# Transposing q and k of batches 3 to 7 through DRAM rows, with loads, shifted copies of v and outputs moved to other queues

## The chip, the cores and the metric

One core of one Trainium2 chip. The metric is the device time of one execution in microseconds (us), as the median of a kernel's runs. The kernel before takes 342.97 us in the first three runs (341.77 to 344.68) and between 341.6 and 343.2 us in the groups of runs used below. Every experiment ran on one chip together with runs of the kernel before. A run is called slow when its time is over 1.5% above the fastest of the same kernel; ratios are of fast runs alone, and differences that only slow runs show are not used. The engines are called PE (TensorE), DVE (VectorE), ACT (ScalarE) and POOL (GpSimd); SP (SyncE) only issues transfers here.

## The reference

Sliding-window attention over 8 batches of 8 heads, 576 positions, head size 64, window 32, and then a two-layer network with an ELU on the 4608 resulting rows:

```python
scores = scale * np.matmul(q, k.transpose(0, 1, 3, 2))     # q, k, v: 8 x 8 x 576 x 64, float32
scores = np.where(np.abs(pos[:, None] - pos[None, :]) <= 32, scores, -1e9)
attn = softmax(scores)
x = np.matmul(attn, v).transpose(0, 2, 1, 3).reshape(4608, 512)
h = x @ w_in                                               # 512 x 2048
out = np.where(h > 0, h, np.exp(np.minimum(h, 0)) - 1) @ w_out
```

## The kernel before

The kernel works in 144 steps. A step is 8 matmuls of the first product and 4 of the second; in the steady part four steps carry one pair of attention blocks (scores, mask, product with v, division by the sums, and a transposing DMA of the result `x_st` into `xT`). The scores are computed from q and k with the head dimension on the partitions (`qT`, `kT`). In the kernel before, TensorE puts them so: a batch's q is loaded as float32 (`f`), cast to bfloat16 (`qkb`), transposed in groups of six (`ptx`) and copied to `qT` or `kT`.

```python
    def load_qk(b, which, part):                 # 1152 KB for a whole q or k of a batch
        ...
        nc.sync.dma_start(out=t[...], in_=(q, k)[which][b, ...])

    def load_v(b, m):                            # five per batch
        nc.gpsimd.dma_start(out=V_e[b % 3][...], in_=v[b, ...])

    def rotate_v(b, m0=0, m1=VS - 1):            # Vo is Ve shifted by 64 partitions
        nc.sync.dma_start(out=o[0:64, m0:m1], in_=e[64:128, m0:m1])
        nc.sync.dma_start(out=o[64:128, m0:m1], in_=e[0:64, m0 + 1:m1 + 1])

    def x_dma(i):                                # 28 pairs; the first 8 use TensorE
        nc.sync.dma_start_transpose(out=xT_of(i), in_=x_st...)
    ...
    for i in range(8, NPAIR):
        kk = 24 if i == 8 else HALF * (i - 2) - 2        # HALF is 4
        at(kk, "mid", scores, i)
        ...
        at(kk + 2, "end", x_dma, i)
    for b in range(2, B):
        k0 = HALF * (first_pair(b) - 2)
        for n in range(2 * HP):
            ...                                          # for b >= 3:
            which, hp = n % 2, n // 2
            kk, ahead = k0 - 16 + HALF * hp + which, 5
            at(kk - ahead, "mid", cast_qk, b, which, WHOLE, (hp,), nc.gpsimd)
            at(kk, "mid", transpose_qk, b, which, WHOLE, (hp,), nc.scalar)
        at(k0 - HALF, "mid", rotate_v, b)
        if b >= 3:
            kk = max(k0 - 8 * HALF, 18)
            at(kk, "mid", load_qk, b, 0, WHOLE)
            at(kk + 1, "mid", load_qk, b, 1, WHOLE)
            for m in range(VS):
                at(kk + 2 + m // 3, "mid", load_v, b, m)
    ...
        if s == STEPS - 1:                               # end of a tile of 256 rows
            nc.scalar.copy(y_sb[:, 0, :], psY[t][0])
            nc.vector.tensor_copy(y_sb[:, 1, :], psY[t][1])
            nc.sync.dma_start(out_t[t], y_sb)
```

`at(step, slot, ...)` puts a task into an engine's program at that step. It is an order, not a time: an engine with nothing to wait for runs ahead of it (in the changed kernel POOL sends out eight transfers, placed at different steps, between 93.45 and 100.08 us).

The softmax here doesn't subtract the row's maximum and nothing guards it: scores larger than these inputs give would overflow.

Of the kernel before, what the change touches and what calls it, by code (L numbers as in the profile page):

```python
# [10 lines left out]
BF16 = mybir.dt.bfloat16  # L11
# [10 lines left out]
def kernel(  # L22
# [9 lines left out]
    nc = tc.nc  # L32
# [13 lines left out]
    SP_ = S // SJ  # L46
    VS = 5
    VD = D + 1
    KW = S + 2 * WIN

    TT = 256
    NT = N_TOK // TT
# [13 lines left out]
    xpool = ctx.enter_context(tc.tile_pool(name="xT", bufs=4))  # L66
    mpool = ctx.enter_context(tc.tile_pool(name="moe", bufs=3))
    opool = ctx.enter_context(tc.tile_pool(name="outs", bufs=2))


    psum = ctx.enter_context(
# [14 lines left out]
        return pools[tag].tile(shape, dt, tag=tag, name=name)  # L86

    qT = [cpool.tile([128, HP, S], BF16, name=f"qT{i}") for i in range(2)]
    kT = [cpool.tile([128, HP, KW], BF16, name=f"kT{i}") for i in range(2)]
    V_e = [cpool.tile([128, VS, H, VD], BF16, name=f"Ve{i}") for i in range(3)]  # L90
    V_o = [cpool.tile([128, VS - 1, H, VD], BF16, name=f"Vo{i}")
           for i in range(3)]
# [6 lines left out]
    WHOLE, HALF_A, HALF_B = (0, SJ), (0, SJ // 2), (1, SJ // 2)  # L99
    qk_f = {}  # L100

    def load_qk(b, which, part):
        z, nj = part
        if (b, which) not in qk_f:
            qk_f[b, which] = lpool.tile([SP_, H * SJ * D], FP32,
                                        tag=f"f{which}", name=f"f{which}")
        t = qk_f[b, which]
        n = H * nj * D
        nc.sync.dma_start(
            out=t[:, z * n:(z + 1) * n].rearrange("p (h x) -> p h x", h=H),  # L110
            in_=(q, k)[which][b, :, z * SP_ * nj:(z + 1) * SP_ * nj, :]
            .rearrange("h (p j) d -> p h (j d)", j=nj))
# [6 lines left out]
            out=V_e[b % 3][p0:p1, m, :, 0:D],  # L119
            in_=v[b, :, lo + p0:lo + p1, :].rearrange("h p d -> p h d"))  # L120

    def rotate_v(b, m0=0, m1=VS - 1):
        e, o = V_e[b % 3], V_o[b % 3]
        nc.sync.dma_start(out=o[0:64, m0:m1], in_=e[64:128, m0:m1])
        nc.sync.dma_start(out=o[64:128, m0:m1], in_=e[0:64, m0 + 1:m1 + 1])

    gate_t = cpool.tile([1, 8], BF16, name="gate_t")
    gates = [0]
# [23 lines left out]
    for i in range(3):  # L152
        nc.vector.memset(V_e[i][:, :, :, D:VD], 1.0)
        nc.vector.memset(V_e[i][0:32, 0], 0.0)
        nc.vector.memset(V_e[i][96:128, VS - 1], 0.0)
        if i < 2:
            nc.vector.memset(kT[i][:, :, 0:WIN], 0.0)
            nc.vector.memset(kT[i][:, :, KW - WIN:KW], 0.0)

    ident = cpool.tile([128, 128], BF16)  # L160
    make_identity(nc, ident)
# [47 lines left out]
    def cast_qk(b, which, part, hps, eng):  # L209
# [8 lines left out]
        qk_b[b, which, z, hp0] = t  # L218
        copy_on(eng, _bap(t, [t.ap[0], [D, nh], [nh * D, nj], [1, D]]), s_)

    def transpose_qk(b, which, part, hps, evac, tag="t0"):
        z, nj = part
        src = qk_b.pop((b, which, z, hps[0]))
        nh = len(hps)
        W = 512 if nh > 1 else 1024
        pt = ps_tile([128, nh, W], BF16, tag, "ptx")
        for g in range(nh):
            for j in range(nj):
                nc.tensor.transpose(  # L229
                    pt[:, g, j * SP_:(j + 1) * SP_],  # L230
                    src[:, j, g * 128:(g + 1) * 128], ident[0:SP_, 0:SP_])
        n = SP_ * nj
        if which == 0:
            T, c0 = qT[b % 2], z * n
        else:
            T, c0 = kT[b % 2], WIN + z * n
        d = T[:, hps[0]:hps[0] + nh, c0:c0 + n]
        pitch = d.ap[1][0] if nh > 1 else n
        copy_on(evac,
                _bap(d, [d.ap[0], [pitch, nh], [nj, SP_], [1, nj]]),  # L240
                _bap(pt, [pt.ap[0], [W, nh], [1, SP_], [SP_, nj]]))
# [3 lines left out]
    def scores(i, tag="s"):  # L245
        psS = ps_tile([128, 2, 512], FP32, tag, "psS")
        for z in range(2):
            jb = 2 * i + z
            b, qb = jb // NQB, jb % NQB
            for h in range(H):  # L250
                hp, base = h // 2, 64 * (h % 2)
                nc.tensor.matmul(  # L252
                    psS[:, h % 2, hp * 128 + z * QB:hp * 128 + (z + 1) * QB],
                    lhsT=kT[b % 2][base:base + 64, hp, QB * qb:QB * qb + 128],
                    rhs=qT[b % 2][base:base + 64, hp, QB * qb:QB * (qb + 1)],
                    start=True, stop=True)
        pu = apool.tile([128, H, 2 * QB], BF16, tag="pu")
# [113 lines left out]
    def at(kk, slot, fn, *args):  # L371
        tasks.setdefault((kk, slot), []).append((fn, args))
# [40 lines left out]
        at(kk + 2, "end", x_dma, i)  # L413
    for b in range(2, B):
        k0 = HALF * (first_pair(b) - 2)
        for n in range(2 * HP):
            if b == 2:
                which, hp, kk, ahead = n // HP, n % HP, 18 + n, 2
            else:
                which, hp = n % 2, n // 2  # L420
                kk, ahead = k0 - 16 + HALF * hp + which, 5
            at(kk - ahead, "mid", cast_qk, b, which, WHOLE, (hp,), nc.gpsimd)
            at(kk, "mid", transpose_qk, b, which, WHOLE, (hp,), nc.scalar)
        at(k0 - HALF, "mid", rotate_v, b)
        if b >= 3:
            kk = max(k0 - 8 * HALF, 18)
            at(kk, "mid", load_qk, b, 0, WHOLE)
            at(kk + 1, "mid", load_qk, b, 1, WHOLE)
            for m in range(VS):
                at(kk + 2 + m // 3, "mid", load_v, b, m)  # L430



# [32 lines left out]
    def mm2(kk):  # L466
# [13 lines left out]
        if s == STEPS - 1:  # L480
            y_sb = opool.tile([128, 2, D_MODEL], FP32, tag="y_sb")
            nc.scalar.copy(y_sb[:, 0, :], psY[t][0])
            nc.vector.tensor_copy(y_sb[:, 1, :], psY[t][1])  # L483
            nc.sync.dma_start(out_t[t], y_sb)

    LAG = 2
    for kk in range(NSTEP + LAG):
# [40 lines left out]
```

## Time and profile before

| | kernel before |
|---|---|
| time, median | 342.97 us |
| span of the profiled run | 339.9 us |
| TensorE (PE) busy | 91%, at full granted clock (1.00 in each window of the prediction) |
| PE's waits for a transfer after 30 us | none over 0.3 us |

The page, the windows and the timeline that bound the kernel are shown in the prediction. Two more views matter for what came of it. First PE's waits (engine, line, what it waited for: us in total, times, longest):

```profile
PE ptx L229 <- DVE qkb L207: 12.5, 4, 7.0
...
PE psS L279 <- DMA Vo<-Ve: 1.9, 1, 1.9
```

Both lie in the start-up. Second, the page's DMA issues (count, size of one, median us from issue to landing):

```profile
f<-in_q_dram SPq DMA_DIRECT2D x6, 1152.0 KB, 9.8
...
Vo<-Ve SPq DMA_DIRECT2D x12, 260.0 KB, 4.0
Ve<-in_v_dram POOLq DMA_DIRECT2D x24, 128.0 KB, 10.9
```

Loads of q and k, the copies `Vo<-Ve` (below: Vo copies), outputs and x transposes are all issued by SP, in program order. SP's timeline (start, duration of the issue, what) shows what that does. I read over it before I predicted:

```profile
98.58 1.19 SPq L317 DMA_TRANSPOSE xT<-x_st  x1
99.87 0.53 SPq L109 DMA_DIRECT2D f<-in_q_dram  x1
106.87 1.19 SPq L317 DMA_TRANSPOSE xT<-x_st  x1
108.15 0.53 SPq L109 DMA_DIRECT2D f<-in_k_dram  x1
```

The program asks for the q load and the k load one step (2 us) apart, but SP stands at an x transpose until `x_st` is there (14 waits, 85.7 us). So in batches 4 and 5 each load leaves 1.3 us after the start of an x transpose's issue, and k 7.9 to 8.3 us after q, behind the next. In batches 6 and 7 that holds for k, which leaves 5.5 to 5.8 us after q; q leaves behind an output, 4.2 to 4.5 us ahead of the next x transpose. Batch 3's two leave at 70.70 and 71.21 us, ahead of all x transposes.

### The profile page before, as it was taken

How to read it: one execution, taken by the hardware profiler on the slowest of the kernel's cores; microseconds unless marked ns; L12 is line 12 of the kernel's file. 1: busy time of each engine (PE TensorE's matmuls, PEld its weight loads, DVE VectorE, ACT ScalarE, POOL GpSimd, SP SyncE). 2: the span in 40 equal slices, each digit the busy share in tenths (PEclk: the TensorE clock that was granted, in tenths of full speed). 3: DMA queues.
4: the chain of work that ended last, by engine and by line, in shares of the span. 5: the costliest groups of instructions: out<-in, count | busy, mean ns of one | idle time of the engine just before them, and what ended most of it. 6: DMA issues, size and time to landing. Idle time of an engine off the chain costs nothing.

```text
span 339.9 us, 8051 instructions
## 1 busy us (share of the span) xinstructions
PE 308.7 (91%) x3296; PEld 207.4 (61%) x3296; DVE 246.2 (72%) x446; ACT 167.3 (49%) x262; POOL 84.3 (25%) x108
## 2 busy tenths in 40 slices
PE   0347999799799999999999999999999999999994
PEld 0235666566566666666666666666666666666662
DVE  5346667678787777778877888788867777878663
ACT  1624264566545554555555554555555553444331
POOL 8352410085661344034400354021100000000000
PEclk9999999999999999999999999999999999999999
DMA  8999999999998995771949994963202320202011
GB/s 163 187 227 214 218 169 185 218 305 214 131 143 173 216 119 121 174 168 23 188 65 206 178 158 83 225 155 80 79 18 78 80 79 17 77 17 80 15 64 62
DMA packets 79176, 45.67 MB, mean 134 GB/s; under 512 B 53796, under 2 KB 73252, under 8 KB 79140
## 3 DMA queue, kind: packets, MB, share of 16 engines
q1 hardware_dynamic: 37412, 36.25, 47.4%
q0 software_dynamic: 41728, 8.92, 37.9%
q8 instruction: 26, 0.43, 0.6%
q14 instruction: 10, 0.08, 0.1%
HBM read 36.70 MB, written 9.44 MB: 136 GB/s over the span
## 4 chain that ended last, share of the span: by engine, by line
PE 83%; DVE 7%; DMA 4%; ACT 3%; issue 1%; SPq 0%; DVEq 0%
PE ps L447 36%; PE psY L474 35%; PE ptx L229 5%; PE psS L279 4%; PE psS L252 3%; DMA f<-in_k_dram 2%; DVE g_sb L460 2%; DMA Vo<-Ve 2%; DVE m_sb L455 1%; ACT e_sb L453 1%; DVE x_st L291 1%; ACT pu L258 1%; ACT qkb L205 1%; DVE pm L267 1%; DVE xT L313 1%
## 5 line engine op out<-in xcount | busy, mean ns | idle before, releaser
L453 ACT ACTIVATE e_sb<-ps 128x512 f32<-128x512 f32 x144 | 86.0, 597 | 152.1 <-PE ps L447 151.9
L447 PE MATMUL ps<-xT,w_in_sb 128*128 128x256 bf16 x1152 | 150.5, 274 | 4.1 <-DVE xT L313 3.3
L474 PE MATMUL psY<-w_out_sb,g_sb 128*128 128x512 bf16 x576 | 148.0, 379 | 0.2 <-DVE g_sb L460 0.2
L447 PEld LDWEIGHTS <-w_in_sb 128*128 128x128 bf16 x1152 | 110.2, 98 | 41.2 <-issue 4.8
L455 DVE TENSOR_SCALAR m_sb<-e_sb 128x512 bf16<-128x512 f32 x144 | 71.9, 500 | 59.2 <-ACT e_sb L453 58.8
L460 DVE SCALAR_TENSOR_TENSOR g_sb<-ps,m_sb 128x512 bf16<-128x512 f32 x144 | 99.4, 690 | 13.0
L474 PEld LDWEIGHTS <-g_sb 128*128 128x128 bf16 x576 | 50.8, 98 | 38.0 <-DVE g_sb L460 0.7
L207 POOL CAST qkb<-f 96x768 bf16<-96x768 f32 x48 | 41.3, 883 | 120.0 <-DMA f<-in_q_dram 40.0
L118 POOL DMA_DIRECT2D Ve<-in_v_dram x40 | 34.8, 875 | 28.1 <-PE psS L279 13.6
L229 PE MATMUL ptx<-ident,qkb 96*128 96x96 bf16 x384 | 27.7, 215 | 15.0 <-DVE qkb L207 12.5
L258 ACT ACTIVATE pu<-psS 128x1024 bf16<-128x1024 f32 x36 | 36.5, 1019 | 2.7 <-PE psS L252 2.6
L229 PEld LDWEIGHTS <-qkb 96*128 96x128 bf16 x384 | 23.5, 102 | 17.3 <-DVE qkb L207 13.0
L267 DVE TENSOR_TENSOR pm<-pu,masks 128x1024 bf16<-128x1024 bf16 x36 | 26.0, 721 | 2.0 <-ACT pu L258 1.7
L291 DVE TENSOR_TENSOR x_st<-psS,rc 128x512 bf16<-128x512 f32 x36 | 24.9, 692 | 1.2
L279 PEld LDWEIGHTS <-pm 128*64 128x64 bf16 x576 | 12.5, 113 | 17.3 <-DVE pm L267 13.4
L205 ACT COPY qT<-ptx 128x576 bf16<-128x576 bf16 (+1 forms) x30 | 20.0, 666 | 4.1 <-PE ptx L229 4.1
L252 PE MATMUL psS<-qT,kT 64*128 64x64 bf16 x576 | 15.3, 196 | 2.7 <-DVE x_st L291 1.2
L205 ACT COPY kT<-ptx 128x576 bf16<-128x576 bf16 (+1 forms) x26 | 17.4, 671 | 0.0
L252 PEld LDWEIGHTS <-kT 64*128 64x128 bf16 x576 | 11.2, 98 | 10.2 <-issue 7.7
L279 PE MATMUL psS<-Ve,pm 128*64 128x65 bf16 x320 | 16.5, 200 | 0.9 <-ACT pu L258 0.6
L279 PE MATMUL psS<-Vo,pm 128*64 128x65 bf16 x256 | 14.5, 200 | 2.0 <-DMA Vo<-Ve 1.9
L483 DVE COPY y_sb<-psY 128x512 f32<-128x512 f32 x18 | 12.4, 687 | 2.2 <-PE psY L474 1.8
(29 smaller groups left out, 55.1 us busy)
## 6 DMA issues: line engine op xcount, KB each, us to landing
out_dram<-y_sb SPq DMA_DIRECT2D x18, 512.0 KB, 2.9
f<-in_q_dram SPq DMA_DIRECT2D x6, 1152.0 KB, 9.8
f<-in_k_dram SPq DMA_DIRECT2D x6, 1152.0 KB, 9.4
Vo<-Ve SPq DMA_DIRECT2D x12, 260.0 KB, 4.0
Ve<-in_v_dram POOLq DMA_DIRECT2D x24, 128.0 KB, 10.9
f<-in_q_dram SPq DMA_DIRECT2D x4, 576.0 KB, 10.3
f<-in_k_dram SPq DMA_DIRECT2D x4, 576.0 KB, 12.0
w_in_sb<-in_moe_w_in_dram POOLq DMA_DIRECT2D x4, 512.0 KB, 19.2
```

Of the source, the lines that this page charges most:

```text
L118: nc.gpsimd.dma_start(out=V_e[b % 3][p0:p1, m, :, 0:D], in_=v[b, :, lo + p0:lo + p1, :].rearrange("h p d -> p h d"))
L205: nc.scalar.copy(d_, s_)
L207: eng.tensor_copy(d_, s_)
L229: nc.tensor.transpose(pt[:, g, j * SP_:(j + 1) * SP_], src[:, j, g * 128:(g + 1) * 128], ident[0:SP_, 0:SP_])
L252: nc.tensor.matmul(psS[:, h % 2, hp * 128 + z * QB:hp * 128 + (z + 1) * QB], lhsT=kT[b % 2][base:base + 64, hp, QB * qb:QB * qb + 128], rh ...
L258: nc.scalar.activation(pu, _bap(psS, [psS.ap[0], [1, 1024]]), AX.Exp, scale=SCALE)
L279: nc.tensor.matmul(psS[QB * z:QB * (z + 1), par, hp * VD:(hp + 1) * VD], lhsT=pm[:, par * HP + hp, z * QB:(z + 1) * QB], rhs=vv[:, qb // 2 ...
L447: nc.tensor.matmul(ps[:, j, :], lhsT=w_in_sb[:, do, fo * 128:(fo + 1) * 128], rhs=xT[t][:, :, do, :], start=(do == 0), stop=(do == NDO - 1))
L453: nc.scalar.activation(e_sb, ps, AX.Exp)
L455: nc.vector.tensor_scalar(m_sb, e_sb, -1.0, None, ALU.add)
L460: nc.vector.scalar_tensor_tensor(g_sb, psH.pop(kk), 0.0, m_t.pop(kk), ALU.max, ALU.min)
L474: nc.tensor.matmul(psY[t][ts], lhsT=g_sb[:, j, ts * 128:(ts + 1) * 128], rhs=w_out_sb[:, s * FG + j, :], start=(s == 0 and j == 0), stop=( ...
```

## The change

The intent is to take the q and k transposes of batches 3 to 7 off TensorE, which bounds the kernel (91% busy). ACT casts `f` to rows in bfloat16 and writes them to DRAM; SP brings them back with a transposing DMA. To keep SP's queue free for transposes, loads of q and k and Vo copies go to POOL's queue, and outputs and row writes to ACT's. ACT also takes over DVE's half of the copies of a finished tile to `y_sb`. (Recorded texts say "output copies" of either: where they go to POOL or hold up a transpose, Vo copies are meant.)

```diff
-    def load_qk(b, which, part):
+    def load_qk(b, which, part, eng=nc.sync):
...
+    def cast_rows(b, which, hp):
+        ...
+        nc.scalar.copy(...)                      # rows <- f, two heads
+    def write_rows(b, which):
+        ...
+        nc.scalar.dma_start(out=t.rearrange("(p j) c -> p j c", j=SJ), in_=rows.pop((b, which)))
+    def transpose_rows(b, which):
+        nc.sync.dma_start_transpose(out=keys_or_queries(b, which), in_=in_dram.pop((b, which)))
...
     for b in range(2, B):
         k0 = HALF * (first_pair(b) - 2)
         ...                                      # b == 2 stays as before
+        k0 -= 2
+        c0 = k0 - (19 if b == 3 else 23)
+        for which in range(2):
+            at(max(c0 - 7, 17) if which == 0 else c0 + 1, "mid",
+               load_qk, b, which, WHOLE, nc.gpsimd)
+            for hp in range(HP):
+                at(c0 + 8 * which + (0, 1, 4, 5)[hp], "end", cast_rows, b, which, hp)
+            at(c0 + 8 * which + 6, "mid", write_rows, b, which)
+            at(c0 + 8 * which + 8, "mid", transpose_rows, b, which)
+        for m in range(VS):
+            at(k0 - 20 + 2 * m, "mid", load_v, b, m)
+        at(k0 - 4, "mid", rotate_v, b, 0, VS - 1, nc.gpsimd)
...
-            nc.vector.tensor_copy(y_sb[:, 1, :], psY[t][1])
-            nc.sync.dma_start(out_t[t], y_sb)
+            nc.scalar.copy(y_sb[:, 1, :], psY[t][1])
+            nc.scalar.dma_start(out_t[t], y_sb)
```

Not shown: `kT` gets one row of positions with padding at its ends, so that one transpose can fill it.

More of the change, by code (lines that the diff above doesn't have):

```diff
@@ L48 @@
     VD = D + 1
-    KW = S + 2 * WIN
     TT = 256
@@ L68 @@
     opool = ctx.enter_context(tc.tile_pool(name="outs", bufs=2))
+    dpool = ctx.enter_context(
+        tc.tile_pool(name="dram", bufs=2, space=bass.MemoryType.DRAM))
     psum = ctx.enter_context(
@@ L88 @@
     qT = [cpool.tile([128, HP, S], BF16, name=f"qT{i}") for i in range(2)]
-    kT = [cpool.tile([128, HP, KW], BF16, name=f"kT{i}") for i in range(2)]
+    KPAD = 2 * WIN
+    kT = [cpool.tile([128, KPAD + HP * S + KPAD], BF16, name=f"kT{i}")
+          for i in range(2)]
     V_e = [cpool.tile([128, VS, H, VD], BF16, name=f"Ve{i}") for i in range(3)]
@@ L108, in load_qk @@
         n = H * nj * D
-        nc.sync.dma_start(
+        eng.dma_start(
             out=t[:, z * n:(z + 1) * n].rearrange("p (h x) -> p h x", h=H),
@@ L120, in load_v, with rotate_v @@
             in_=v[b, :, lo + p0:lo + p1, :].rearrange("h p d -> p h d"))
-    def rotate_v(b, m0=0, m1=VS - 1):
+    def rotate_v(b, m0=0, m1=VS - 1, eng=nc.sync):
         e, o = V_e[b % 3], V_o[b % 3]
-        nc.sync.dma_start(out=o[0:64, m0:m1], in_=e[64:128, m0:m1])
-        nc.sync.dma_start(out=o[64:128, m0:m1], in_=e[0:64, m0 + 1:m1 + 1])
+        eng.dma_start(out=o[0:64, m0:m1], in_=e[64:128, m0:m1])
+        eng.dma_start(out=o[64:128, m0:m1], in_=e[0:64, m0 + 1:m1 + 1])
     gate_t = cpool.tile([1, 8], BF16, name="gate_t")
@@ L156 @@
         if i < 2:
-            nc.vector.memset(kT[i][:, :, 0:WIN], 0.0)
-            nc.vector.memset(kT[i][:, :, KW - WIN:KW], 0.0)
+            for c0, n in ((KPAD - WIN, HP), (KPAD + HP * S, 1)):
+                z = kT[i][:, c0:c0 + WIN]
+                nc.vector.memset(_bap(z, [z.ap[0], [S, n], [1, WIN]]), 0.0)
     ident = cpool.tile([128, 128], BF16)
@@ L219, in cast_qk, with keys_or_queries @@
         copy_on(eng, _bap(t, [t.ap[0], [D, nh], [nh * D, nj], [1, D]]), s_)
+    def keys_or_queries(b, which):
+        if which == 0:
+            return qT[b % 2]
+        return kT[b % 2][:, KPAD:KPAD + HP * S].rearrange(
+            "p (g s) -> p g s", g=HP)
+    rows, in_dram = {}, {}
+    def cast_rows(b, which, hp):
+        if hp == 0:
+            rows[b, which] = lpool.tile([SP_, SJ, H * D], BF16,
+                                        tag=f"r{which}", name="rows", bufs=1)
+        n = SJ * D
+        s_ = qk_f[b, which][:, 2 * hp * n:(2 * hp + 2) * n]
+        d_ = rows[b, which][:, :, 2 * hp * D:(2 * hp + 2) * D]
+        nc.scalar.copy(
+            _bap(d_, [d_.ap[0], [D, 2], [H * D, SJ], [1, D]]),
+            _bap(s_, [s_.ap[0], [n, 2], [D, SJ], [1, D]]))
+    def write_rows(b, which):
+        t = dpool.tile([S, H * D], BF16, tag=f"d{which}", name="in_dram")
+        in_dram[b, which] = t
+        nc.scalar.dma_start(
+            out=t.rearrange("(p j) c -> p j c", j=SJ), in_=rows.pop((b, which)))
+    def transpose_rows(b, which):
+        nc.sync.dma_start_transpose(
+            out=keys_or_queries(b, which), in_=in_dram.pop((b, which)))
     def transpose_qk(b, which, part, hps, evac, tag="t0"):
@@ L232, in transpose_qk @@
         n = SP_ * nj
-        if which == 0:
-            T, c0 = qT[b % 2], z * n
-        else:
-            T, c0 = kT[b % 2], WIN + z * n
-        d = T[:, hps[0]:hps[0] + nh, c0:c0 + n]
+        d = keys_or_queries(b, which)[:, hps[0]:hps[0] + nh, z * n:(z + 1) * n]
         pitch = d.ap[1][0] if nh > 1 else n
@@ L253, in scores @@
                     psS[:, h % 2, hp * 128 + z * QB:hp * 128 + (z + 1) * QB],
-                    lhsT=kT[b % 2][base:base + 64, hp, QB * qb:QB * qb + 128],
+                    lhsT=kT[b % 2][base:base + 64, KPAD + hp * S + QB * qb - WIN:
+                                   KPAD + hp * S + QB * qb - WIN + 128],
                     rhs=qT[b % 2][base:base + 64, hp, QB * qb:QB * (qb + 1)],
@@ L415 @@
         k0 = HALF * (first_pair(b) - 2)
-        for n in range(2 * HP):
-            if b == 2:
-                which, hp, kk, ahead = n // HP, n % HP, 18 + n, 2
-            else:
-                which, hp = n % 2, n // 2
-                kk, ahead = k0 - 16 + HALF * hp + which, 5
-            at(kk - ahead, "mid", cast_qk, b, which, WHOLE, (hp,), nc.gpsimd)
-            at(kk, "mid", transpose_qk, b, which, WHOLE, (hp,), nc.scalar)
-        at(k0 - HALF, "mid", rotate_v, b)
-        if b >= 3:
-            kk = max(k0 - 8 * HALF, 18)
-            at(kk, "mid", load_qk, b, 0, WHOLE)
-            at(kk + 1, "mid", load_qk, b, 1, WHOLE)
-            for m in range(VS):
-                at(kk + 2 + m // 3, "mid", load_v, b, m)
+        if b == 2:
+            for n in range(2 * HP):
+                which, hp = n // HP, n % HP
+                at(16 + n, "mid", cast_qk, b, which, WHOLE, (hp,), nc.gpsimd)
+                at(18 + n, "mid", transpose_qk, b, which, WHOLE, (hp,),
+                   nc.scalar)
+            at(k0 - HALF, "mid", rotate_v, b)
+            continue
+        k0 -= 2
[4 more added lines that the diff above has]
+            for hp in range(HP):
+                at(c0 + 8 * which + (0, 1, 4, 5)[hp], "end",
+                   cast_rows, b, which, hp)
+            at(c0 + 8 * which + 6, "mid", write_rows, b, which)
[3 more added lines that the diff above has]
+        at(k0 - 4, "mid", rotate_v, b, 0, VS - 1, nc.gpsimd)
     order = [(z, n) for z in range(2) for n in range(HALF)]
```

## The prediction

> **What bounds the kernel now.** I read the page first. TensorE (PE) is busy 91% of the span at full granted clock, and the chain of work that ended last runs mostly on it:
>
> ```profile
> PE 308.7 (91%) x3296; PEld 207.4 (61%) x3296; DVE 246.2 (72%) x446; ACT 167.3 (49%) x262; POOL 84.3 (25%) x108
> PE   0347999799799999999999999999999999999994
> PE 83%; DVE 7%; DMA 4%; ACT 3%; issue 1%; SPq 0%; DVEq 0%
> ```
>
> A busy PE is a hint only, because matmul ends are modelled. So I looked at the period of the schedule in the table of windows. The kernel issues 144 steps (a step is 8 matmuls of the first product and 4 of the second). Four steps carry one attention pair (scores and PV). While batches 3 to 7 are prepared, two of those four also carry a group of six TensorE transposes of q or k. One four-step period with such groups, then one without, then two from near the end (all start and end where a product's matmuls start):
>
> ```profile
> 96.85:105.25 8.40, 8.40 (x99) 5.67 (x93) 6.31 (x12) 4.36 (x7) 2.21 (x3) 1.00 1.60 145
> 130.43:138.30 7.87, 7.87 (x86) 5.16 (x80) 6.24 (x11) 3.30 (x5) 3.40 (x4) 1.00 0.75 136
> 288.71:296.59 7.88, 7.88 (x83) 5.15 (x82) 6.38 (x13) 3.78 (x6) 0.00 (x0) 1.00 0.26 83
> 296.59:304.48 7.89, 7.89 (x82) 5.17 (x82) 5.89 (x12) 3.30 (x5) 0.00 (x0) 1.00 0.09 19
> ```
>
> Columns: stretch, its length, busy PE, PEld, DVE, ACT, POOL, clock, DMA share, GB/s. PE fills every period; DVE has 1.5 to 2 us free, ACT over 3.5. The period is the same at DMA share 0.09 and 0.75, so no transfer paces it. From about 95 us on the kernel is bound by PE's instruction stream, and time that leaves the stream should leave the span. Between 27 and 95 us PE also waits, 0.5 to 1.9 us at a time, for DVE or ACT.
>
> [...]
> [...]
> - [...] the 131 KB of an x transpose pass as 512 packets of 256 bytes, 18 ns each, over 0.75 us, or 175 GB/s.
> - [...] So a row write's landing lies in series with each new transpose. The trace of before has no such pair.
> - [...] `m_sb` takes 0.43 us alone and 0.83 us where a POOL cast runs (at 156.8 and 158.8 us).
>
> **The change, part by part.**
>
> (1) Removed from PE: for five batches 8 groups of six transposes. Per period the saving is 8.40 - 7.88 = 0.52 us for two groups, 0.26 each (the 27.7 us of the ptx row are overlapping modelled spans and not used). 40 x 0.26 = 10.4 us, all of it in the PE-bound stretch. This is the ceiling of this part, 3.0% of 343.
>
> (2) ACT loses 40 evacuations and gains 40 casts, 18 second output copies and 28 DMA issues (10 row writes, 18 outputs). Rows used:
>
> ```profile
> L205 ACT COPY qT<-ptx 128x576 bf16<-128x576 bf16 x28 | 17.8, 634 | 3.8 <-PE ptx L229 3.8
> L205 ACT CAST qkb<-f 96x768 bf16<-96x768 f32 x4 | 3.3, 829 | 2.8 <-DMA f<-in_k_dram 2.8
> L482 ACT COPY y_sb<-psY 128x512 f32<-128x512 f32 x18 | 10.8, 597 | 2.0 <-PE psY L474 2.0
> L483 DVE COPY y_sb<-psY 128x512 f32<-128x512 f32 x18 | 12.4, 687 | 2.2 <-PE psY L474 1.8
> ```
>
> -40 x 0.634 + 40 x 0.829 + 18 x 0.597 + 28 x 0.45 (SP's issue of an output takes 0.38 to 0.41, of other loads about 0.5) = -25.4 + 33.2 + 10.7 + 12.6 = +31 us: 167 becomes about 198 of 335. Not a bound by sum. In order, what counts is whether an exp comes late. A cast after an exp ends 1.43 us into a 1.74 us step and costs nothing. The output step does. In the timeline before, copies and exps stand so:
>
> ```profile
> 291.96 0.58 ACT L482 COPY y_sb<-psY 128x512 f32<-128x512 f32 x1
> 292.44 0.68 DVE L483 COPY y_sb<-psY 128x512 f32<-128x512 f32 x1
> 293.20 0.60 ACT L453 ACTIVATE e_sb<-ps 128x512 f32<-128x512 f32 x1 [0.66 <-PE ps L447]
> 293.70 1.02 ACT L258 ACTIVATE pu<-psS 128x1024 bf16<-128x1024 f32 x1
> 294.97 0.68 DVE L267 TENSOR_TENSOR pm<-pu,masks 128x1024 bf16<-128x1024 bf16 x1
> ```
>
> The second copy on ACT ends near 293.1, the output issue near 293.55: the exp comes 0.35 us later, and the mask (`pm`) too. It ended at 295.65 and PE took it up at 296.14, so this just fits; I allow 0.05 us in 14 tiles, 0.7 us. In batches 6 and 7 four row writes fall in the same step as an output, 0.5 us more each: 2 us. For tiles 0 and 1 both copies precede a 1.12 us evacuation, and PE waits there already for ACT (0.83 us at 70.28): +0.9 us. Sum: -3.6 us of the gain.
>
> (3) POOL loses 40 casts of 0.82 us (8 stay) and issues loads and Vo copies. DVE is no longer held up by them, and loses 12 us of copies. Little of it is on the path: the 1.2 us that PE waits for x_st at 92 us, where five POOL casts stretch `pm` to 1.28 us, should go. +1.2 us.
>
> (4) New transfers: per batch two writes of 590 KB (like the 512 KB output, 2.9 us to landing; with more traffic I take 4 to 5) and two transposes of 590 KB.
>
> ```profile
> L317 SPq DMA_TRANSPOSE xT<-x_st x28: 1189/1191/1549, 93.4 to 313.9; - x28
> DMA to landing us min/median/max: 2.4/3.4/6.4
> ```
>
> A new transpose has 4.5 times the bytes of an x transpose: 4.5 x 0.75 = 3.4 us of packets, with start and end about 5 us, estimated 4.5 to 7 beside other traffic. The schedule gives k of batches 4 to 7 seven steps (13 us) between the transpose's issue slot and its first scores: enough. k of batch 3 has three steps. Its write goes out in step 37 and lands 4.5 to 5.5 us later; the transpose lands at +9.5 to +12; scores of step 42 come at +9.6 (5 x 1.74 + 0.9). I take -1.0 us. In batches 6 and 7 the new transpose (steps 83, 91, 99, 107) precedes on SP the x transpose of an odd pair, due 13 us after the write's issue; it lands at +11.5 to +13.5. I take -0.7 us in all.
>
> Sum: 10.4 + 1.2 - 3.6 - 1.0 - 0.7 = 6.3 us, so 336.7. I chose somewhat better, 335.5, as the schedule (casts placed beside the pair steps, k of batch 3 brought forward) looks tuned on the chip, which my allowances for ACT do not know.
>
> **The rivals.**
> - A: PE's stream is the bound and everything new hides. 343 - 10.4 - 1.2 = 331.4. For it: the same period at every DMA share. Against: the tight places in (2) and (4).
> - B: ACT turns into a wait. If a DMA issue on ACT takes 1 us or more, for instance while SP's large transpose is being issued, the exp after each output is late by another 0.5 us: 16 x 0.5 = 8 us back, 340 to 341. Against: SP's issues of outputs take 0.4 us; but for SP the trace also shows single issues of 2 to 3.5 us[...].
> - C: transfers become the bound. From 100 to 220 us the DMA share is 0.5 to 1.1 already. If a transpose takes over 10 us, x transposes behind it come late, 4 times about 4 us, and batch 3 waits 5 us: 348. Against: the x transposes' 18 ns packets.
>
> **How the range and chances follow.** A gives 331.4, my sum 336.7, B 340.5; 80% between 331 and 341. Faster by over 2% means under 336.1, which needs two thirds of the PE saving; my number is just beyond it, so it is nearly a coin's throw, with a lean to faster. Slower by over 2% needs C in full.
>
> **What would show each step.** (1) Right if periods of four steps during batches 3 to 7 last 7.9 us, and ptx matmuls fall from 384 to 144. (2) Right if ACT stays near 60% busy, its output issues take about 0.45 us, and PE's waits for `pm`, ACT's `y_sb` and `e_sb` after 100 us stay under 3 us in total; wrong if they recur in each tile. (3) Right if the wait near 92 us is gone. (4) Right if the new transposes land in 4.5 to 7 us and PE waits once, 0 to 3 us, for kT of batch 3; wrong if PE waits for xT behind a new transpose. The whole is wrong if PE is the bound no longer, or if periods without groups grow past 7.9 us.

## The result

The changed kernel takes **382.44 us** (380.49 to 384.86, 4 runs) against 342.37 us of the kernel before (341.70 to 344.68, 4 runs): ratio 1.116, 95% interval 1.1076 to 1.1245. It is slower by 40 us. (A ratio is the mean time of one kernel's fast runs over that of the other's fast runs of the same rounds, so it isn't quite the ratio of the medians.) The result is correct, and the profiled run is a fast one.

The page of the changed kernel, by the rows that the prediction showed of before (busy times, PE's forty slices, the chain that ended last), with the row of the granted clock:

```profile
PE 305.3 (80%) x3056; PEld 200.0 (52%) x3056; DVE 227.9 (59%) x428; ACT 183.5 (48%) x280; POOL 62.9 (16%) x88
...
PE   0458998898909930998089999199999999999995
...
PEclk9999999999968995899579999589999999999998
...
PE 62%; DMA 24%; DVE 6%; ACT 4%; issue 2%; ACTq 0%; SPq 0%; DVEq 0%
```

PE's row now has four holes, and the granted clock drops in each (the trace's clock record goes from 1.0 to 0.5 at 108, 142, 183 and 241 us). The chain spends 24% on transfers instead of 4%. PE's waits name them:

```profile
PE psS L284 <- DMA kT<-in_dram: 23.9, 2, 15.1
...
PE ps L486 <- DMA xT<-x_st: 22.8, 2, 11.8
```

These four waits are 46.7 us. The chain in order of time gives the transfers behind them (start, us, what), and what PE did after each:

```profile
98.20 17.24 DMA xT<-x_st
115.58 1.86 PE ps L486 x8
...
133.06 19.29 DMA kT<-in_dram
...
178.62 14.11 DMA xT<-x_st
...
226.06 21.51 DMA kT<-in_dram
```

An x transpose of 17 us, where 6.4 us was the longest before; and the first of them was issued at 98.20 us, while the first transpose from DRAM was issued at 115.20. So the new transposes can't have caused the first hole. After a hole PE needs 1.86 us for eight matmuls that take 0.87 elsewhere in the same chain. The windows (stretch, length, busy PE, PEld, DVE, ACT, POOL, clock, DMA share, GB/s) show the clock in the first hole, just after it, and in an undisturbed period:

```profile
104.50:115.58 11.08, 0.04 (x4) 0.03 (x1) 1.49 (x3) 0.14 (x1) 0.78 (x1) 0.66 1.76 203
115.58:118.74 3.16, 3.16 (x14) 1.82 (x15) 0.53 (x2) 1.26 (x2) 0.00 (x0) 0.59 1.65 200
...
200.51:208.39 7.88, 7.88 (x83) 5.17 (x81) 6.11 (x13) 5.08 (x8) 1.56 (x2) 1.00 0.48 124
```

Where nothing stalls, a period of four steps takes 7.88 us, as the prediction said. The landings, from the page, with the medians of before in mind:

```profile
f<-in_q_dram POOLq DMA_DIRECT2D x5, 1152.0 KB, 13.4
...
Ve<-in_v_dram POOLq DMA_DIRECT2D x24, 128.0 KB, 19.3
Vo<-Ve POOLq DMA_DIRECT2D x10, 260.0 KB, 13.6
```

Everything lands later: outputs 4.6 instead of 2.9 us (by the same rows), q 13.4 instead of 9.8, v 19.3 instead of 10.9, Vo 13.6 instead of 4.0. By tile, the transposes from DRAM landed in 4.8 to 20.6 us (median 9.7), and the x transposes in 2.4 to 19.6 (median 4.7, before 3.4). The issue of a transpose from DRAM kept SP for 2.2 to 12.0 us, that of an x transpose for 1.19 at the median.

POOL's timeline ahead of the first hole shows the last piece:

```profile
93.45 0.73 POOL L129 DMA_DIRECT2D Vo<-Ve  x1 [11.24 <-DMA Ve<-in_v_dram]
...
94.69 0.82 POOL L114 DMA_DIRECT2D f<-in_k_dram  x1
95.50 3.43 POOL L123 DMA_DIRECT2D Ve<-in_v_dram  x4
99.28 0.80 POOL L114 DMA_DIRECT2D f<-in_q_dram  x1 [0.35 <-ACT rows L243]
```

Within 7 us POOL sends out two loads, four v loads and both Vo copies: nothing in POOL's program waits for the step in which they were placed, only for data and free buffers (the bracket gives the idle time before, and what ended it).

One thing does not fit a queue that is merely full. From 98 to 102 us, while two x transposes were on their way, the DMA engines moved only 43 GB/s (203 in the hole itself). In and around that stretch 30 packets of the Vo copies took over 1 us each, most of them about 3 us; the median in this run is 0.31, and the kernel before has none over 1 us. What held them is not known, and no run tests it.

### The profile page after: what moved, and what is told of

It reads as the page before. It is cut to its first block, busy times and chain, and to the rows that moved or that the text cites. A ratio compares the mean times of both kernels' runs of the same rounds, so it can differ in the third digit from the quotient of the medians.

```text
span 383.2 us, 7528 instructions
## 1 busy us (share of the span) xinstructions
PE 305.3 (80%) x3056; PEld 200.0 (52%) x3056; DVE 227.9 (59%) x428; ACT 183.5 (48%) x280; POOL 62.9 (16%) x88
## 4 chain that ended last, share of the span: by engine, by line
PE 62%; DMA 24%; DVE 6%; ACT 4%; issue 2%; ACTq 0%; SPq 0%; DVEq 0%
PE ps L486 29%; PE psY L513 27%; DMA kT<-in_dram 11%; DMA xT<-x_st 8%; PE psS L312 3%; PE psS L284 3%; DMA f<-in_k_dram 2%; DVE g_sb L499 2%; ACT e_sb L492 2%; DMA Vo<-Ve 2%; DVE m_sb L494 1%; DMA in_dram<-rows 1%; PE ptx L265 1%; DVE x_st L324 1%; DVE pm L300 1%
## 5 line engine op out<-in xcount | busy, mean ns | idle before, releaser
L486 PE MATMUL ps<-xT,w_in_sb 128*128 128x256 bf16 x1152 | 153.9, 278 | 27.9 <-DMA xT<-x_st 22.8
L513 PE MATMUL psY<-w_out_sb,g_sb 128*128 128x512 bf16 x576 | 151.1, 386 | 0.2 <-DVE g_sb L499 0.2
L486 PEld LDWEIGHTS <-w_in_sb 128*128 128x128 bf16 x1152 | 111.9, 100 | 67.3 <-issue 18.5
L494 DVE TENSOR_SCALAR m_sb<-e_sb 128x512 bf16<-128x512 f32 x144 | 63.4, 440 | 79.9 <-ACT e_sb L492 79.5
L513 PEld LDWEIGHTS <-g_sb 128*128 128x128 bf16 x576 | 53.9, 99 | 40.4 <-issue 2.2
L243 ACT CAST rows<-f 96x768 bf16<-96x768 f32 x40 | 32.8, 821 | 0.0
L284 PEld LDWEIGHTS <-kT 64*128 64x128 bf16 x576 | 11.4, 99 | 33.4 <-DMA kT<-in_dram 24.1
L265 PE MATMUL ptx<-ident,qkb 96*128 96x96 bf16 x144 | 10.8, 230 | 15.1 <-DVE qkb L213 12.9
L265 PEld LDWEIGHTS <-qkb 96*128 96x128 bf16 x144 | 8.8, 111 | 16.5 <-DVE qkb L213 13.4
L114 POOL DMA_DIRECT2D f<-in_k_dram x5 | 4.0, 797 | 49.0 <-ACT rows L243 49.0
L521 ACT COPY y_sb<-psY 128x512 f32<-128x512 f32 x18 | 10.5, 585 | 2.0 <-PE psY L513 2.0
L522 ACT COPY y_sb<-psY 128x512 f32<-128x512 f32 x18 | 10.9, 603 | 0.0
## 6 DMA issues: line engine op xcount, KB each, us to landing
f<-in_q_dram POOLq DMA_DIRECT2D x5, 1152.0 KB, 13.4
Ve<-in_v_dram POOLq DMA_DIRECT2D x24, 128.0 KB, 19.3
Vo<-Ve POOLq DMA_DIRECT2D x10, 260.0 KB, 13.6
```

The costliest lines, as they stand in the source:

```text
L243: nc.scalar.copy(_bap(d_, [d_.ap[0], [D, 2], [H * D, SJ], [1, D]]), _bap(s_, [s_.ap[0], [n, 2], [D, SJ], [1, D]]))
L284: nc.tensor.matmul(psS[:, h % 2, hp * 128 + z * QB:hp * 128 + (z + 1) * QB], lhsT=kT[b % 2][base:base + 64, KPAD + hp * S + QB * qb - WIN: ...
L486: nc.tensor.matmul(ps[:, j, :], lhsT=w_in_sb[:, do, fo * 128:(fo + 1) * 128], rhs=xT[t][:, :, do, :], start=(do == 0), stop=(do == NDO - 1))
L494: nc.vector.tensor_scalar(m_sb, e_sb, -1.0, None, ALU.add)
L513: nc.tensor.matmul(psY[t][ts], lhsT=g_sb[:, j, ts * 128:(ts + 1) * 128], rhs=w_out_sb[:, s * FG + j, :], start=(s == 0 and j == 0), stop=( ...
```

## The experiments

Two parts of the change can be undone apart: the **path** (rows in DRAM instead of TensorE) and the **queues** (who issues loads, Vo copies and outputs). Theory Q: loads on another queue than SP's make the x transposes late. Theory P: the path itself costs, by bytes or by time. Theory order: each is a matter of what stands in front of a transpose. Where I say "by the packets" below, I took the trace's records of single packets: a transpose goes as packets of 256 bytes in SP's queue (512 for one of x, 2304 for one from DRAM), and I dealt them out in order of start to the transposes in order of issue. Several expectations speak of packets that take turns: in e3's trace, from 102 to 105 us, 128 packets of an x transpose and 130 of 4608 bytes from POOL's queue started side by side. That turns cost time was a theory of mine, which no run shows.

### Loads on SP's and on ACT's queue (e1, e2)

```diff
-               load_qk, b, which, WHOLE, nc.gpsimd)
+               load_qk, b, which, WHOLE, nc.sync)        # e2: nc.scalar
```

> The changed kernel with one thing undone: the loads of q and k of batches 3 to 7 go on SP's queue again instead of POOL's. Theory Q (the loads on POOL's queue hold up the transposes[...]): 332 to 340 us, new transposes land in 4 to 7 us. Theory P (the new path itself is slow: large transposes from DRAM crawl beside any other traffic): 370 to 385 us, landing stays at about 10 us median.

> The changed kernel with the loads of q and k of batches 3 to 7 on ACT's queue. Theory Q in the form that only POOL's software queue does harm: 332 to 342 us. Theory Q in the form that any queue beside SP's does it: 360 to 385, transposes still land in about 10 us. Theory P: 370 to 385.

e1: 359.77 us median (354.11 to 360.63, 4 runs). Only the run of 354.11 is a fast one and the profiled run is slow, so I give no ratio and don't use its details. It lies outside both expected ranges. e2: 375.77 us, ratio 1.0964 (1.0879 to 1.105). With the loads back on SP some 28 us of the 40 are gone by that one fast run; with the loads on ACT's queue only 7. So the loads' queue is a large part, and it isn't POOL alone that hurts: a queue besides SP's does. ACT's time for issuing is not the trouble: its DMA issues took 0.34 to 0.42 us in the changed kernel, but for one of 0.95.

### The queues alone and the path alone (e3, e4, e8)

e3 is the kernel before with the changed queues; e8 the same with the loads left on SP; e4 is the changed kernel with all queues as before, row writes on ACT.

```diff
 # e3, against the kernel before
-            at(kk, "mid", load_qk, b, 0, WHOLE)
-            at(kk + 1, "mid", load_qk, b, 1, WHOLE)
+            at(kk, "mid", load_qk, b, 0, WHOLE, nc.gpsimd)        # e8 leaves these two
+            at(kk + 1, "mid", load_qk, b, 1, WHOLE, nc.gpsimd)
 # and: rotate_v on nc.gpsimd for b > 2, second copy to y_sb and output on nc.scalar
 # e4, against the changed kernel: loads, rotate_v and outputs on nc.sync, second copy to y_sb on nc.vector
```

> The kernel before (TensorE transposes of q and k kept, no DRAM rows) with only the queues moved: loads and Vo copies of batches 3 to 7 on POOL's queue, outputs and both output copies on ACT. Theory Q: the x transposes come late, 352 to 385 us. Theory P: 340 to 348 us.

> The new path alone: q and k through DRAM rows and DMA transposes, but loads, Vo copies and outputs on SP's queue and the second output copy on DVE, as in the kernel before. Theory Q: 332 to 342 us. Theory P: 365 to 385 us.

> e3_queues_only with the loads back on SP: the kernel before with only Vo copies on POOL's queue, outputs and the second output copy on ACT. If the loads on POOL's queue are what costs in e3 (packet by packet alternation with 4608-byte packets): 340 to 346 us. If splitting the traffic over three queues costs in itself: 352 us or more.

| | time us | ratio (95%) | PE's wait for xT | x landing, median / max |
|---|---|---|---|---|
| before | 342 | 1 | 0 | 3.4 / 6.4 |
| e8, outputs and Vo moved | 345.28 | 1.0097 (1.0031 to 1.0164) | 0 | 3.3 / 7.8 |
| e3, and loads on POOL | 358.94 | 1.0462 (1.0381 to 1.0543) | 9.0 | 4.0 / 14.7 |
| e4, path alone | 355.98 | 1.0382 (1.031 to 1.0454) | 10.1 | 4.0 / 10.4 |
| changed kernel | 382.44 | 1.116 (1.1076 to 1.1245) | 22.8 | 4.7 / 19.6 |

Both parts cost by themselves, and together more than the sum (3.8% and 4.6% make 8.4%, measured 11.6%). Of the queues' 4.6%, 3.7 are the loads on POOL (e3 against e8). e3 came out as theory Q expected, and e8 as expected if the loads are what costs; e4 lies between its two ranges, so neither theory had it right.

### The path with its order mended (e5, e6, e7)

In e4 PE waits for x transposes that stand in SP's queue behind bulk. SP's timeline of e4 around one of them (the two Vo copies are left out; the last line merges two transposes, of which the first, with 2.65 us of issue, landed after 10.4 us):

```profile
201.89 1.39 SPq L523 DMA_DIRECT2D out_dram<-y_sb  x1
...
204.87 1.12 SPq L114 DMA_DIRECT2D f<-in_k_dram  x1
206.08 8.81 SPq L350 DMA_TRANSPOSE xT<-x_st  x2
```

e5 moves loads, row writes and transposes so that each follows an x transpose, where 8 us are free. e6 leaves e4's order and issues the pairs from 14 on up to four steps sooner, so that a late transpose has more slack; e7 does the same to the changed kernel.

```diff
 # e5, against e4
-        c0 = k0 - (19 if b == 3 else 23)
+        c0 = {3: 23, 4: 37, 5: 53, 6: 77, 7: 93}[b]
...          # loads at c0 - 8 + 8 * which (b == 3: 17, 21), transposes ahead of them in the step
 # e6, e7
-        kk = 24 if i == 8 else HALF * (i - 2) - 2
+        kk = 24 if i == 8 else HALF * (i - 2) - 2 - min(4, max(0, i - 13))
...          # the loads, casts, writes and transposes of a batch move with its first pair
```

> e4_path_only with the same work spaced otherwise: the large issues on SP (new transposes, loads of q and k of batches 4 to 7) moved to the step just after the x transpose of an odd pair, which is the urgent one. Theory Order (in e4 the x transposes lose their margin because a load or a new transpose stands just ahead of them in SP's queue): 332 to 341 us, PE's waits for xT under 3 us. Theory Full (the DMA engines have no time left in batches 3 to 7): 350 us or more, waits only move.

> e4_path_only with the pairs from number 14 on up to four steps earlier (and with them all work of batches 4 to 7), so that an odd pair's x transpose has eight steps instead of four. Theory Margin (only the time to landing is too long for the margin): 331 to 338 us, no wait for xT after 160 us. Theory Full: 350 us or more.

> The changed kernel with the pairs from number 14 on up to four steps earlier, as in e6. Theory Margin: the waits for xT in batches 4 to 7 go, those for kT stay (their margin is unchanged): 345 to 368 us. Theory Full: 378 us or more.

e5: 343.77 us, ratio 1.0037 (0.9978 to 1.0096). e6: 347.0 us, 1.0064 (0.9948 to 1.018). Both lie between the ranges of their two theories. Still, of the path's 13 us about 12 were order (e5), or some 11 lack of slack (e6), and theory P falls: the bytes are the same. e7: 381.08 us, 1.1088 (1.099 to 1.1185; its profiled run is slow), in the range of theory Full: slack doesn't help while the loads are on POOL. What is left in e5 is one long wait (for xT it was 1.1 us in all):

```profile
PE psS L284 <- DMA kT<-in_dram: 8.1, 1, 8.1
```

It is k of batch 3, whose transpose was issued at 120.73, behind a load (114.76) and two Vo copies. The granted clock was 0.74 on average from 120 to 140 us, and 1.00 in the 20 us after.

### Taking out the last wait (e9, e10, e15)

e9 casts, writes and transposes k of batch 3 sooner, ahead of that load and those copies. e10 leaves batch 3 to TensorE and uses the path for batches 4 to 7 only. e15 is e10 with Vo copies and v loads of batches 4 to 7 two steps sooner.

```diff
 # e9, against e5: batch 3 only
+            tr = (31, 37)[which] if b == 3 else c0 + 8 + w
+            wr = (29, 34)[which] if b == 3 else c0 + 6 + w
...          # its casts in steps 23, 24, 27, 28 and 29, 31, 32, 33; rotate_v one step sooner
 # e10, against e5
+        if b == 3:
+            ...                    # casts on POOL, TensorE's transposes, loads as in the kernel before
+            continue
 # e15, against e10
-            at(k0 - 20 + 2 * m, "mid", load_v, b, m)
-        at(k0 - 4, "mid", rotate_v, b)
+            at(k0 - 22 + 2 * m, "mid", load_v, b, m)
+        at(k0 - 6, "mid", rotate_v, b)
```

> e5_path_spaced with k of batch 3 cast, written and transposed earlier, ahead of the loads and output copies that held it up. Theory order (what is left in e5 is the one wait for kT of batch 3, 8.1 us, and the half-speed clock after it): 331 to 337 us, the kT wait under 2 us. Rival (the path costs its time in other ways, such as packets and ACT's writes, and the wait only moves): 341 us or more, with another wait of similar size in the table of waits.

> e5_path_spaced with q and k of batch 3 transposed on TensorE as before, the DRAM path for batches 4 to 7 only. 32 groups of six transposes at 0.26 us are 8.3 us less than before. Theory order: 333 to 337 us, no kT wait over 2 us. Rival (the path costs as much as it saves wherever it is): 341 us or more.

> e10_path_pe3 with the copies Vo<-Ve of batches 4 to 7, and the loads they wait for, two steps earlier. If the wait for Vo (4.4 us in two places, one of them near the start and as in the kernel before) can be had back in part: 331 to 334 us. If the copies only collide with a transpose instead: 335 us or more.

e9: 337.31 us (336.25 to 339.71), ratio 0.9845 (0.9776 to 0.9913). e10: **335.13 us** (334.37 to 336.17) against 343.19 of the kernel before in the same rounds, ratio 0.9774 (0.9727 to 0.9821). Both beat both kernels. e10 takes 32 groups of transposes off PE, and 32 x 0.26 = 8.3 us was what the prediction's unit gives; the medians differ by 8.1. That is closer than it should be, for e10 also waits 2.5 us longer for Vo (4.4 instead of 1.9) and 0.4 for xT. The spans of the profiled runs fit the whole sum: 8.3 - 2.5 - 0.4 = 5.4, measured 339.9 - 334.4 = 5.5. e9 takes 40 off (10.4) and gains 5.9; PE's waits say where some of the rest went, first e9's, then e10's:

```profile
PE ps L490 <- DMA xT<-x_st: 4.4, 4, 1.7
```

```profile
PE ps L499 <- DMA xT<-x_st: 0.4, 1, 0.4
```

In e10 x transposes still land as late as 8.9 us, and PE waits 0.4 us for them: here lateness cost only past the slack. e9's expected range just misses (337.3 where 337 was its end). e15 gave 336.51 us, 0.9837 (0.9786 to 0.9888), in other rounds: no gain shown, as its second branch expected.

### Why loads on POOL's queue cost: first round (e11, e12)

e11 is e5's order with the changed kernel's queues. e12 adds, ahead of each load on POOL, a tiny copy that waits for a DVE memset of that step, so that POOL can't run ahead.

```diff
 # e11, against e5: loads and rotate_v on nc.gpsimd, outputs and their second copy on nc.scalar
 # e12, against e11
+    def pace():
+        nc.vector.memset(pace_t[:, n:n + 1], 0.0)
+        nc.gpsimd.tensor_copy(pace_p[:, n:n + 1], pace_t[:, n:n + 1])
+            at(ld, "mid", pace)
             at(ld, "mid", load_qk, b, which, WHOLE, nc.gpsimd)
```

> The changed kernel with its own queues (loads and output copies on POOL, outputs and row writes on ACT), but with the steps of e5_path_spaced. Theory Q (loads on POOL's queue hurt by themselves, since POOL runs ahead and its packets take turns with the transposes' packets): 360 us or more, landings of the x transposes up to 12 us and more. Rival (order of the schedule alone was wrong): 342 to 348 us as e5.

> e11_after_spaced with each load on POOL held back to its step by a small copy that waits for VectorE. If POOL running ahead is what makes its queue costly: 338 to 348 us. If the taking of turns, one packet of 4608 bytes for each of the transposes' 256, hurts wherever it falls: 355 us or more, with landings of the x transposes still over 10 us.

e11: 385.63 us, ratio 1.1209 (1.1128 to 1.1291): the order that mends the path does nothing with the loads on POOL. e12: 369.8 us, 1.0674 (1.0565 to 1.0784; two of its four runs are slow and not in the ratio). By the ratios, holding POOL back gives some 18 us of 41, and 23 remain. By their marks e11's theory Q and e12's second branch came true (x landings of up to 18.1 and 20.6 us); POOL's running ahead is a part, and whether turns of packets are the rest these runs don't show.

### Second round: packet size, a miss (e13, e14)

I thought that a 256-byte packet of a transpose waits for one of POOL's packets of 4608 bytes (SP's loads went as 1536), so that its landing follows their size; no run shows that. Halving each load was to make POOL's packets smaller, in e3 (e13) and in e12 (e14).

```diff
-        eng.dma_start(out=dst, in_=src)
+        for i in range(2):
+            eng.dma_start(out=dst[:, :, i * w:(i + 1) * w], in_=src[:, :, i * w:(i + 1) * w])
```

> e3_queues_only (TensorE's transposes, loads on POOL's queue) with each load on POOL's queue issued as two halves of 768-byte runs, so that it goes in smaller packets than 4608 bytes. Theory turns[...]: landings of the x transposes at most about 8 us instead of 14.7, waits for xT under 4 us instead of 9.0, time 346 to 354 us instead of 358.9. Rival (what counts is bytes in flight or POOL running ahead, not the packet's size): landings of 12 us and more and a time of 356 us or more, as e3.

> e12_after_paced (whole change, loads on POOL's queue held back to their step) with the same halving of the loads. Theory turns, with POOL running ahead already taken away: 346 to 358 us instead of 369.8, landings of the transposes from DRAM under 12 us at most. Rival (packet size does not matter): 364 us or more, kT waits of 10 us and more.

e13: 361.91 us, 1.0544 (1.0458 to 1.063). e14: 372.06 us, but three of its four runs are slow, the profiled one too, and the fast one took 365.05. Neither tests anything: by the packets, the loads of both still went as 2560 packets of 4608 bytes, as e3's did. The expectation rested on a premise that the run didn't meet.

### Third round: where the load stands (e16, e17, e18)

SP's timeline of before (shown above) had another candidate: there the two loads of a batch left 5.5 to 8.3 us apart from batch 4 on, and six of those eight 1.3 us behind an x transpose. e16 is e3 with the loads held back on POOL to that place (q right after one x transpose, k after the next, with the pacing of e12). e17 puts them at the same steps on ACT's queue. e18 is e8 with both loads asked for in one step on SP. In e16 and e17 the v loads also moved two steps later.

```diff
 # e16, against e3
-            at(kk, "mid", load_qk, b, 0, WHOLE, nc.gpsimd)
-            at(kk + 1, "mid", load_qk, b, 1, WHOLE, nc.gpsimd)
+            for which in range(2):
+                ks = max(kk - HALF, 17) + HALF * which
+                at(ks, "end", pace)                          # not in e17
+                at(ks, "end", load_qk, b, which, WHOLE, nc.gpsimd)      # e17: nc.scalar
 # e18, against e8
-            at(kk + 1, "mid", load_qk, b, 1, WHOLE)
+            at(kk, "mid", load_qk, b, 1, WHOLE)
```

> e3_queues_only (TensorE's transposes, loads on POOL's queue), with each load held back on POOL to where it stood on SP's queue in the kernel before: q right after one x transpose, k right after the next, four steps later. Theory timing (on SP's queue a load stood behind an x transpose and so was spaced; on POOL both went at once and early): waits for xT under 3 us, 344 to 349 us instead of 358.9. Theory turns (a load on a queue of its own shares the engines with the x transpose packet by packet whenever it is issued): 354 us or more.

> e3_queues_only with the loads on ACT's queue at the same steps as in e16_queues_spaced. Theory timing: as e16, 344 to 350 us. Theory turns by packet size (ACT's queue sends 1536-byte packets, POOL's 4608): better than e16 by 4 us or more, with the x transposes' landings at most 9 us.

> e8_outs_vo_only (loads on SP's queue, 345.3 us) with both loads of a batch issued at once, one behind the other in SP's queue, as POOL issued them. Theory timing[...]: 350 us or more, waits for xT of 5 us and more. Theory turns (only a queue of their own hurts): 344 to 347 us.

e16: 354.05 us, 1.0316 (1.0243 to 1.0388). e17: 366.9 us, 1.0648 (1.0541 to 1.0754). e18: 348.41 us, 1.0147 (1.0084 to 1.021). Timing as I put it falls short: by the ratios, spacing gives back only some 5 us of e3's 16 and leaves e16 at the very edge of what the other theory expected (354). Bunching on SP's queue costs 2 to 3 us over e8 if anything (the intervals of the ratios overlap), between the two expectations. Packet size alone explains it no better: ACT's packets are 1536 bytes, and e17, which misses both its expectations, is the slowest of the three. (That is no clean test of the size, as its loads stood elsewhere.) What the three traces do show is finer than the steps that I set. On ACT the load of e17 left just ahead of the x transpose after all; ACT's issue in the timeline, and the x transpose in the chain:

```profile
98.63 0.32 ACTq L109 DMA_DIRECT2D f<-in_q_dram  x1
```

```profile
99.42 9.35 DMA xT<-x_st
```

In e16 it stands the other way round (SP's, then POOL's timeline):

```profile
97.58 1.20 SPq L317 DMA_TRANSPOSE xT<-x_st  x1
```

```profile
98.77 0.79 POOL L109 DMA_DIRECT2D f<-in_q_dram  x1 [0.37 <-issue]
```

By the packets, e16's x transpose had its last packet start 2.1 us after its issue, with none of POOL's or ACT's in between, and it landed after 4.1 us. e17's had its *first* packet 5.6 us after its issue, once 1173 KB of other queues had gone (a whole load is 1152), and its last at 8.4 us. The load stood 0.8 us ahead of the transpose in the one and 1.2 us behind it in the other, and the landing took 9.35 us or 4.1. The two also differ in the load's queue and its packets; but on POOL's queue, too, a load ahead goes with a late transpose: in e3 the q load left 2.0 us ahead of the x transpose of 95.30 us, which landed after 14.7.

The same count for all x transposes (28 in each kernel; first and last are us from the issue to the start of the first and last packet; undisturbed they are 1.17 and 1.93):

| kernel | with the first packet later than 3 us | latest first | latest last |
|---|---|---|---|
| before | 0 | 2.3 | 4.6 |
| e8, loads on SP | 2 | 3.1 | 5.5 |
| e18, both at once on SP | 5 | 6.1 | 7.7 |
| e16, POOL held to its place | 4 | 5.4 | 9.1 |
| e17, the same steps on ACT | 7 | 6.1 | 10.4 |
| e3, POOL | 8 | 6.7 | 11.9 |
| changed kernel | 9 | 11.4 | 15.7 |

(Where two transposes are in flight at once, dealing packets out in order is rough: by it the changed kernel's x transpose of 93.17 us started its last packet at 102.6, but it landed at 112.7.)

In e3 five of its eight late ones had 1341 to 1421 KB of other queues' packets ahead of their first, the other three about 800 to 920 KB. In e16 all four have 450 to 733 KB ahead, in some 3500 to 4400 packets, nearly all of them v loads (128 bytes each). So part of what e16 leaves over e8 is, as far as the trace tells, v loads that now stand in front of an x transpose; no run took them away. PE waits 4.3 us for xT there, but also 3.5 us for DVE's `pm` (e8: none and 0.6), which was not followed up.

In the changed kernel eight of the nine late ones also had 299 to 443 KB of SP's own queue ahead, that is, of other transposes: there the path's large transposes did stand in front. The ninth, issued at 98.20 us, had only 166 KB of other queues ahead in its 4.5 us; it falls into the stretch of 43 GB/s.

In the two stretches that I counted, a transpose's packets and another queue's started in about equal numbers, as if by turns. In the changed kernel, from 110 to 112 us, 316 packets of the x transpose and 314 of POOL's queue started (269 of these of 128 bytes, 31 of 4608); alone, the 512 packets pass in 0.76 us. In e3, from 102 to 105 us, it was 128 of the x transpose and 130 of 4608 bytes, each of which took 0.34 us; whether the size of a packet counts there is not shown, as no run changed it. That doesn't explain the 5 us before the first packet, which the trace shows and for which I have no tested reason.

## Why the prediction was wrong, point by point

**Step (1), PE's saving: right.** ptx matmuls fell from 384 to 144, an undisturbed period took 7.88 us, and the unit of 0.26 us held in e10 (its span fits to 0.1 us once its longer waits are taken off).

**Step (2), ACT: right in what it excluded, close in size.** ACT's busy time was 183.5 us where the step's sum gives 186 without the issues, which the page does not count as busy. ACT's issues took 0.34 to 0.42 us (one 0.95), and PE's waits for ACT's `y_sb` and DVE's `pm` added up to 2.4 us. The +0.9 us for tiles 0 and 1 came true: PE waited 1.7 us for `y_sb` instead of 0.8. Rival B fell. Moving outputs, their copies and Vo without the loads costs 1.0% (e8), some 3.3 us. The step allowed 3.6, but 2.0 of these were for row writes, which e8 doesn't have, so the likeness is in part luck.

**Step (3), relief for POOL and DVE: this is where the sum lacks a term.** It counted what POOL no longer does, +1.2 us (the wait near 92 us did fall, from 1.2 to 0.5), and gave no cost at all to "POOL issues loads and Vo copies". That term is 3.7% alone (e3 against e8), some 13 us, and more with the path. Six of the ten loads on SP's queue had left 1.3 us behind an x transpose, where SP had stood until `x_st` was there; on POOL only data and free buffers held them (ACT's `rows`: 6 waits, 74.5 us in the changed kernel). (Holding them there, e16, gave back some 5 us of e3's 16; the v loads behind them moved too, so that the rest isn't apportioned.)

**Step (4), transfers: the failed step.** "Estimated 4.5 to 7 beside other traffic" was the packets of one x transpose, scaled by bytes, which leaves out what stands in front. Measured in the changed kernel: 4.8 to 20.6, median 9.7. For k of batch 3 the row write took as long as was said (its transpose went out 5.5 us later), but the transpose landed after 19.3 us. The x transposes, for which it took -0.7 us in all, stood at 2.4 to 19.6. Two mis-sized terms, then: k of batch 3 was -1.0 and measured 15.1, the longer of the two waits for kT (the other, 8.8, was not in the sum at all); x was -0.7 and measured 22.8. After each hole PE was also slow for 3.2 to 3.9 us (granted clock 0.59, 0.55, 0.50 and 0.52); after the first, eight plus four matmuls took 3.16 us where 1.73 is normal (0.87 + 0.86), so some 1.4 us for that hole and, as an estimate, about 6 for four, a cost that the prediction didn't have. 46.7 + 6 - 10.4 = 42 us, against 43.3 us between the two profiled spans. The estimate itself was good for a transpose that leaves with nothing in front: in e10, where order is kept, the new ones landed in 4.6 to 6.5 us. One reading beside this step was wrong: the trace of before does have transfers that read what another wrote. The Vo copies read what the v loads wrote, and SP waited 25.9 us for these in all. In the changed kernel SP waited ten times for row writes ahead of the new transposes, 57.3 us in all.

**Rival C was the right kind and the wrong size.** It said that x transposes come late behind transposes of over 10 us and gave 348 us. (Its own terms make more: 4 x 4 + 5 = 21 us on top of A's 331.4 are 352.) Lateness there was, but the first hole came before any transpose from DRAM was issued, and the four waits were 8.8 to 15.1 us long, not 4 to 5. Later ones did stand behind such transposes, and behind other queues' loads besides. I argued against it with "the x transposes' 18 ns packets": a packet's own time says nothing about what stands in front of it. The DMA share of "0.5 to 1.1" between 100 and 220 us was noted and not followed to its question: whose packets, issued when, ahead of what?

**The closing hunch failed too.** I shaved 1.2 us off because the schedule "looks tuned on the chip". The schedule with its loads on SP (e1) and the path alone on SP (e4) were slow as well.

**What stays open.** Why a transpose's first packet waits, in five of e3's eight and in e17, for about a load's worth of other queues' packets, where in the stretches counted the queues' packets started in about equal numbers; what held the DMA engines to 43 GB/s ahead of the first hole; how the interplay of path and queues makes 3 points more than their sum; and what the v loads alone cost in e16.

## What to carry to other kernels

Before moving transfers to another engine's queue, look at what the old queue's program order did for them. In the kernel before, SP's waits for `x_st` ahead of an x transpose (85.7 us) also held back, for nothing, the loads behind it. A load that then went out 0.8 us ahead of the urgent transfer instead of 1.2 us behind it went with a landing after 9.35 us instead of 4.1 in the pair compared here. In this kernel it paid to place bulk transfers right behind an urgent small one, with the time to the next as their budget (e5: 343.77 us, e4: 355.98), rather than to give them a queue of their own (e3: 358.94 us, e8: 345.28). Where the order was right, the change's idea was worth what was first computed for it (e10: 2.3% faster).
